# Routed attention and a gated MLP on one core: the second maxima step's mask pass beside the scores in 32-row tiles, `bounded` next to `shifted`, and the routing maxima in the score bank

## The chip, the cores and the metric

The kernel runs on one core of a Trainium2 chip. The metric is the time of one execution in device microseconds (us). A measurement of it can tell about 0.2% from no change. The engines are named as in the profile: PE (TensorE matmuls; PEld its weight loads), DVE (VectorE), ACT (ScalarE), POOL (GpSimd), SP (SyncE, which issues DMAs).

## The reference

Two blocks in a row. The first is attention with routing: queries and keys are each assigned to the nearest of 16 centroids of their head (by cosine), and a query attends only to keys of its own cluster. The second is an MLP whose hidden layer is gated by `h * erf(softplus(h))`.

```python
# q, k, v: (4, 8, 768, 64); centroids: (8, 16, 64); float32
q_assign = argmax(einsum('bhsd,hcd->bhsc', normed(q), normed(centroids)), -1)
k_assign = argmax(einsum('bhsd,hcd->bhsc', normed(k), normed(centroids)), -1)
scores = where(q_assign[..., :, None] == k_assign[..., None, :], q @ k.T / sqrt(64), -1e9)
attn = exp(scores - scores.max(-1)); attn /= attn.sum(-1) + 1e-9
x = (attn @ v) as (3072, 512)
h = x @ w_in                                  # (512, 2048)
out = (h * erf(softplus(h))) @ w_out          # (2048, 512)
```

## The kernel before

The first 420 us or so are attention, the rest is the MLP (a Strassen-like scheme of seven block products, which the diff does not touch). The weights of the MLP are loaded during attention as 64-bit words whose conversion to float is done by hand, step by step, on ACT, DVE and POOL.

**Pairs, units, periods.** Attention works on 16 pairs of heads. The two heads e = 0, 1 of a pair lie on partitions 0 to 63 and 64 to 127, so each matmul on one head uses a 64-row tile of the array and the two heads' matmuls can stand side by side. A pair has 12 units: `half` (384 of the 768 queries) times `j` (a tile of 128 keys). One call of `period(p, i)` emits two units, `u` and `u + 1`; a pair has six periods, i = 0 to 5. Instructions issued through `te`, `ve`, `ae`, `ge` stay on their engine in the order in which the program emits them; the DMAs on `nc.sync` are placed by the scheduler.

**What a period emits on PE, in order.** At i = 0 and 3 first `turn` (six small matmuls that turn the row minima). Then the first maxima step `step_ahead(u)`; `products(u)` and `products(u + 1)` (f32, `qT` by `kT`, into two banks of a tile named `sc`); the second maxima step `step_ahead(u + 1)`; `scores(u)` and `scores(u + 1)` (bf16, `qm` by `km`, added onto the products); at i = 3 the `similarities` of the pair after next; and `attend` of the two units of the period before (f32, `pr` by `v`, into a bank named `turned`). ACT's `curve` takes the exponential of an `sc` tile into `pr`. There are two `sc` tiles, used in turn.

**Masks.** For each head, `km` and `qm` (bf16, 64 rows by 768) hold, in rows 0 to 15, a penalty of -BIG for each cluster that is not the key's, and a one for the query's cluster; in row 32 (`SH`), a one for the key and the shift of the query. Their product is the mask plus the shift, so `scores` adds both at once. `pick` spreads the one-hot rows `hotT` into these places (`masks`), and `nbig` is the bias of the `km` conversion. `MASKS` says in which periods, and at which of four places in a period, a mask is made.

**Maxima.** A maxima step (12 for each pair, made half a pair ahead) gives an upper bound of the masked scores of 128 queries over 384 keys: two passes into the tile `wide` (two banks, one for each head; there is a single such tile), first `qv` by `kv` (bf16 copies of q and k), then `qm` by `km`, the mask; DVE reduces `wide` over its 768 columns into `nmx`. After six steps DVE reduces `nmx` into `lowest`, and `turn` brings the result into row 32 of `qm`. The next step can overwrite `wide` only after the reduction.

**Routing.** `choose` runs in period 3: DVE transposes the similarities into `sims`, reduces each group of 16 to its maximum `mx`, which stands in 24 spare columns (488 to 511) of `wide`'s first bank, compares (`hot`), and in period 5 transposes `hot` into `hotT`.

**Weights.** For each of 22 early weight pieces: ACT's `size_and_rest`, DVE's `bounded` (a maximum with 2.0), DVE's `shifted` (a shift by 3) with ACT's `sign`, POOL's `summed`. Two pieces are in work in each pair.

In the profile all instructions carry the line of the recording helper (L63), so groups are told apart by the names of their tiles: `wide<-kv,qv` and `wide<-km,qm` are the passes of the maxima steps, `sc<-qT,kT` (or `sc<-more_out`, every third pair, whose q and k lie in `more_out`) the products, `sc<-qm,km` the scores, `turned<-pr,in_v` the attends, `turned<-hotT,pick` a mask, `turned<-lowest,identb` the warming matmuls of the set-up.

Of the kernel before, what the change touches and what calls it, by code (L numbers as in the profile page):

```python
# [20 lines left out]
B, H, S, D = 4, 8, 768, 64  # L21
C = 16
NJ = S // P
Q = 32
# [4 lines left out]
NPAIR = B * HP  # L29
# [14 lines left out]
BIG = 2.0**60  # L44
FLOOR = 2.0**50
EPS = 2.0**-70
SH = 2 * C
NPT = NJ + 2
N_LATE = 10
LAST_X = 11  # L50
# [21 lines left out]
def kernel(  # L72
# [168 lines left out]
    def bounded(n):  # L241
        w = w_steps[n][0]
        ve.tensor_scalar(out=w, in0=w, scalar1=2.0, scalar2=None, op0=ALU.max)
# [5 lines left out]
    def shifted(n):  # L249
        w = w_steps[n][0].bitcast(U32)  # L250
        ve.tensor_scalar(out=w, in0=w, scalar1=3, scalar2=None, op0=ALU.logical_shift_left)
# [6 lines left out]

    ve.memset(nbig, 0.0)
    for e in range(2):  # L260
        ve.memset(nbig[e * D : e * D + C], -BIG)
        ve.memset(nbig[e * D + SH : e * D + SH + 1], 1.0)
    for t in maxima:
        ve.memset(t, FLOOR)
    ve.memset(pick, 0.0)
# [58 lines left out]
    def choose(p, spare=None):  # L324

        if p >= NPAIR:
            return
        st = pairs[p]
        n = HW // C
        sims = routep.tile([P, HW], F32, name="sims")  # L330
        ve.transpose(out=sims, in_=st.pop("psim"))
        yield
        sim = sims.rearrange("p (g c) -> p g c", c=C)
        mx = (wide[:, 0] if spare is None else spare)[:, 512 - n :]
        ve.reduce_max(out=mx, in_=sim, axis=AX.X)
        yield
        hot = routep.tile([P, HW], BF16, name="hot")
        ve.tensor_tensor(
            out=hot.rearrange("p (g c) -> p g c", c=C), in0=sim,
            in1=mx.unsqueeze(2).to_broadcast([P, n, C]), op=ALU.is_equal,  # L340
        )
        yield
        st["hotT"] = routep.tile([P, HW], BF16, name="hotT")
        ve.transpose(out=st["hotT"], in_=hot)
# [2 lines left out]
        if p < NPAIR:  # L347
            ae.copy(out=pairs[p][nm + "v"], in_=pairs[p][nm + "T"])

    def masks(p, nm, half, bank):  # L350

        if p >= NPAIR:
            return lambda: None
        st = pairs[p]
        cols = slice(half * HW, (half + 1) * HW)
        r = slice(0, D) if nm == "q" else slice(D, P)
        won = bank[:, 0:HW]
        te.matmul(won, lhsT=pick[r, half], rhs=st["hotT"][r], start=True, stop=True)
        if nm == "q":
            return lambda: ae.activation(out=st["qm"][:, cols], in_=won, func=ACT.Relu)  # L360
        return lambda: ae.activation(
            out=st["km"][:, cols], in_=won, func=ACT.Identity, bias=nbig, scale=BIG
        )

    turns = []

    def maxima_step(p, i, sm=wide):

        st = pairs[p]
        nmx = maxima[p % 2]  # L370
        t, half = divmod(i, 2)
        for a, b, start in (("qv", "kv", True), ("qm", "km", False)):
            for e in range(2):
                r = slice(e * D, (e + 1) * D)
                te.matmul(
                    sm[:, e, 0:HW], lhsT=st[a][r, t * P : (t + 1) * P],
                    rhs=st[b][r, half * HW : (half + 1) * HW], start=start, stop=not start,
                )
        ve.tensor_reduce(
            out=nmx[:, :, t, half], in_=sm[:, :, 0:HW], axis=AX.X, op=ALU.max, negate=True  # L380
        )
        if i in (NJ - 1, 2 * NJ - 1):
            h = i // NJ
            ve.tensor_reduce(
                out=lowest[h][:, :, SH::D].rearrange("p t e -> p e t"),
                in_=nmx[:, :, h * HJ : (h + 1) * HJ], axis=AX.X, op=ALU.min,
            )
            turns.append((p, h))

    def turn(p, h, copies=(ae.copy, ae.copy)):  # L390

        st = pairs[p]
        pn = turned[h][:, 0:HW].rearrange("p (t n) -> p t n", t=HJ)
        for t in range(HJ):
            for e in range(2):
                cols = slice(e * D, (e + 1) * D)
                te.matmul(pn[cols, t], lhsT=lowest[h][:, t, cols], rhs=identb, start=True, stop=True)
        for e, copy in zip(range(2), copies):
            r = slice(e * D + SH, e * D + SH + 1)
            copy(out=st["qm"][r, h * HW : (h + 1) * HW], in_=pn[r].rearrange("p t n -> p (t n)"))  # L400
        st["shift", h] = True

# [20 lines left out]
    def scores(u):  # L423

        p, half, j = units[u]
        st = pairs[p]
        sc = sc_of[u]
        assert ("shift", half) in st
        for e in range(2):
            r = slice(e * D, (e + 1) * D)  # L430
            te.matmul(
                sc[:, e, 0:HW], lhsT=st["km"][r, j * P : (j + 1) * P],
                rhs=st["qm"][r, half * HW : (half + 1) * HW], start=False, stop=True,
            )
# [270 lines left out]
    def run(work):  # L705
        for _ in work:
            pass

    def step_ahead(u):
        p, i = divmod(u + NJ, 2 * NJ)
        if p < NPAIR:
            maxima_step(p, i)

    forms = sum((left_forms(ve, *w_in_parts(f, 2)) for f in range(0, HF, 2)), [])
    routing = [iter(())]
# [2 lines left out]
    def period(p, i):  # L720
        u = 2 * NJ * p + 2 * i
        n1, n2 = 2 * p - 1, 2 * p
        early = lambda n: 0 <= n < N_EARLY

        def mask(place):
            which = (MASKS if p else FIRST_MASKS).get((i, place))
            if which:
                return masks(p + 1, *which, turned[0 if i in (0, 5) else 1])
            return lambda: None

        if u > 0:
            for which in turns if i in (0, 3) else ():
                turn(*which)
                turns.remove(which)
            step_ahead(u)
        mask(0)()
        next(part[0], None)
        if u == 2:
            next(routing[0])
        products(u)  # L740
        products(u + 1)
        mask(1)()
        if u > 0:
            step_ahead(u + 1)
        next(part[0], None)
        scores(u)
        scores(u + 1)
        later = mask(2)
        if i == 3:
            similarities(p + 2)  # L750
            routing[0] = choose(p + 2)
        curve(u)
        later()
        curve(u + 1)
        if u == 0:
            step_ahead(1)
            similarities(1)
            routing[0] = choose(1, turned[0])
            next(routing[0])
            next(routing[0])  # L760
            vectors(1, "q")
            vectors(1, "k")
        if i == 0 and early(n1 - 1):
            shifted(n1 - 1)
            sign(n1 - 1)
        elif i == 1 and early(n1):
            size_and_rest(n1)
        elif i == 2 and early(n1):
            bounded(n1)
        elif i == 3 and early(n1):  # L770
            shifted(n1)
            sign(n1)
        elif i == 4 and early(n2):
            size_and_rest(n2)
        elif i == 5 and early(n2):
            bounded(n2)
        for work in forms[: FORMS.get(p, {}).get(i, 0)]:
            work()
            forms.remove(work)
        if i == 3:  # L780
            for _ in range(3):
                next(routing[0], None)
        if i == 0:
            if p:
                transposes(p + 2, "q")
        elif i == 1:
            load(p + 1, "v", v, vp)
            if p == 0:
                run(routing[0])
                transposes(2, "q")  # L790
        elif i == 2:
            transposes(p + 2, "k")
        elif i == 4:
            vectors(p + 2, "k")
        elif i == 5:
            run(routing[0])
            vectors(p + 2, "q")
        if u > 0:
            for w in (u - 2, u - 1):
                accumulate(w)  # L800
            if i == 1 and early(n1 - 1):
                summed(n1 - 1)
            elif i == 4 and early(n1):
                summed(n1)
            for w in (u - 2, u - 1):
                attend(w)
            if i % HJ == 0:
                part[0] = divide(u - 1)
                next(part[0])
        mask(3)()  # L810
# [25 lines left out]
    for r in (0, D):  # L836
        for half in range(2):
            for e in range(2):
                c = r + half * Q + e * C
                ve.tensor_copy(  # L840
                    out=pick[r : r + D, half, e * D : e * D + C], in_=first[r : r + D, c : c + C]
                )
    also = ps_s.tile([P, 2, 512], F32, name="sc", tag="s")
    products(0)
# [11 lines left out]
    for n in range(PLACES - 1):  # L856
        fetch(n)
    for i in range(NJ):
        maxima_step(0, i, also if i % 2 else wide)
        if i == 1:  # L860
            masks(0, "q", 1, turned[1])()
        if i < NJ - 1:
            warm(2, turned[0], zeros)
# [125 lines left out]
```

## Time and profile before

| | |
|---|---|
| time, median of 3 runs | 1015.37 us (1015.36 to 1015.42) |
| the profiled execution: time, span | 1015.54 us, 1013.8 us |
| granted PE clock | 1.000 |
| busy: PE, PEld, DVE, ACT, POOL | 1006.4, 724.0, 695.5, 513.5, 346.5 us |
| `wide<-kv,qv` 64*128 64x384 bf16 | x378, 69.4 us busy |
| `wide<-km,qm` 64*128 64x384 bf16 | x378, 68.3 us busy |
| `sc<-qm,km` 64*128 64x384 bf16 | x384, 53.7 us busy |
| 46 to 342 us: busy DVE, ACT, POOL of 296 us | 228.75, 236.47, 227.76 us |

A shape such as 64*128 is the tile of the array (rows by columns), 64x384 the moving operand. Busy times count an overlap of two matmuls once. The ends of matmuls are modelled, so the distance between starts says more than a length. "Waits" are the times in which an engine stood idle before an instruction that a semaphore of another engine released last.

### The profile page before, as it was taken

The page shows a single profiled execution, that of the slowest core. Times are in us where ns is not written, and L with a number is a line of the kernel's source. Part 1 is how long each engine was busy: PE and PEld are TensorE (multiplying, and loading weights), DVE is VectorE, ACT ScalarE, POOL GpSimd, SP SyncE. Part 2 cuts the span into 40 slices and gives each one's busy share as a digit, 9 for nine tenths or more (in the row PEclk, how much of TensorE's full clock was granted, in tenths as well). Part 3 has the DMA queues.
Part 4 walks back from the last instruction along what each step waited for, and adds up shares of the span by engine and source line. Part 5 has one row for each costly group of instructions (what it writes and reads, how often), then busy time and mean ns, then how long its engine had stood idle before and what let it go on. Part 6 is the DMA issues. An engine that isn't in the chain of part 4 may idle for free.

```text
span 1013.8 us, 15440 instructions
## 1 busy us (share of the span) xinstructions
PE 1006.4 (99%) x5930; PEld 724.0 (71%) x5930; DVE 695.5 (69%) x1305; ACT 513.5 (51%) x673; POOL 346.5 (34%) x229
## 2 busy tenths in 40 slices
PE   8999999999999999999999999999999999999998
PEld 3555555555555555488888888888888888888887
DVE  8777777777777777879766564756565647565753
ACT  3788888888887666467714232222324150505050
POOL 1777777777777667844030000000000000000000
PEclk9999999999999999999999999999999999999999
DMA  9344444444344311052000100110001000000001
GB/s 218 67 103 100 99 103 104 105 105 105 83 105 104 63 32 33 16 174 68 17 1 33 51 1 1 42 42 1 18 24 42 1 22 22 1 1 21 21 1 41
DMA packets 141641, 55.55 MB, mean 55 GB/s; under 512 B 127104, under 2 KB 131456, under 8 KB 141568
## 3 DMA queue, kind: packets, MB, share of 16 engines
q1 hardware_dynamic: 139216, 54.28, 20.9%
q8 instruction: 46, 0.75, 0.3%
q10 hardware_dynamic: 2352, 0.30, 0.2%
q14 instruction: 27, 0.22, 0.1%
HBM read 41.98 MB, written 12.58 MB: 54 GB/s over the span
## 4 chain that ended last, share of the span: by engine, by line
PE 97%; DVE 1%; DMA 1%; POOL 0%; ACT 0%; SPq 0%; issue 0%; DVEq 0%; ACTq 0%; POOLq 0%
PE bank L63 43%; PE turned L63 32%; PE sc L63 15%; PE wide L63 7%; DVE nmx L63 1%; POOL more_out L63 0%; DMA in_k<-in_k_dram 0%; DMA in_q<-in_q_dram 0%; DVE kT L63 0%; SPq L63 0%; DVE sims L63 0%; ACT inv L63 0%; DVE qT L63 0%; ACT pr L63 0%; DVE den L63 0%
## 5 line engine op out<-in xcount | busy, mean ns | idle before, releaser
L63 POOL TENSOR_TENSOR more_out<-more_out,pr 128x768 f32<-128x768 f32 x128 | 224.0, 1750 | 68.0 <-ACT pr L63 62.9
L63 DVE TENSOR_REDUCE nmx<-wide 128x2 f32<-128x768 f32 x189 | 180.7, 956 | 88.6 <-PE wide L63 64.3
L63 ACT ACTIVATE pr<-sc 128x768 f32<-128x768 f32 x192 | 147.1, 810 | 78.1 <-PE sc L63 78.1
L63 PE MATMUL turned<-pr,in_v 128*64 128x386 f32 x768 | 145.4, 500 | 0.1
L63 DVE TENSOR_TENSOR g<-bank,g 128x256 f32<-128x256 f32 x222 | 89.5, 421 | 53.2 <-PE bank L63 46.7
L63 PE MATMUL bank<-x_own,w_in 128*128 128x256 f32 x424 | 104.5, 380 | 0.0
L63 PE MATMUL bank<-w_out,g 128*128 128x256 f32 x448 | 103.1, 379 | 0.0
L63 PE MATMUL sc<-qT,kT 64*128 64x384 f32 x528 | 99.7, 484 | 0.0
L63 PEld LDWEIGHTS turned<-pr,in_v 128*64 128x64 f32 x768 | 46.6, 136 | 69.8 <-issue 65.1
L63 PEld LDWEIGHTS bank<-w_out,g 128*128 128x128 f32 x448 | 85.1, 190 | 11.6
L63 PEld LDWEIGHTS bank<-x_own,w_in 128*128 128x128 f32 x424 | 80.3, 190 | 12.2 <-issue 1.2
L63 ACT COPY g<-bank 128x256 f32<-128x256 f32 x28 | 10.4, 372 | 152.2 <-PE bank L63 148.2
L63 DVE TENSOR_TENSOR osb<-bank,osb 128x256 f32<-128x256 f32 x87 | 35.4, 419 | 72.8 <-ACT osb L63 25.4
L63 ACT ACT_TABLE_LOAD x48 | 61.6, 1283 | 45.9 <-DVE g L63 40.9
L63 POOL TENSOR_TENSOR more_out<-pr,pr 128x768 f32<-128x768 f32 x32 | 59.1, 1847 | 50.0 <-ACT pr L63 38.5
L63 PE MATMUL bank<-x_more,more_in 128*128 128x256 f32 x296 | 76.0, 379 | 0.0
L63 PEld LDWEIGHTS <-qv 64*128 64x128 bf16 x384 | 25.6, 93 | 65.2 <-issue 51.0
L63 PE MATMUL wide<-kv,qv 64*128 64x384 bf16 x378 | 69.4, 328 | 1.1 <-ACT km L63 0.6
L63 PE MATMUL wide<-km,qm 64*128 64x384 bf16 x378 | 68.3, 322 | 0.0
L63 PEld LDWEIGHTS sc<-qT,kT 64*128 64x128 f32 x528 | 56.2, 187 | 16.6 <-issue 1.2
L63 PE MATMUL bank<-more_out,g_more 128*128 128x256 f32 x272 | 64.3, 379 | 0.0
L63 DVE TENSOR_TENSOR g<-a_s,g 128x512 f32<-128x512 f32 x96 | 62.4, 687 | 1.4 <-ACT a_s L63 1.4
(162 smaller groups left out, 1704.8 us busy)
## 6 DMA issues: line engine op xcount, KB each, us to landing
x_own<-in_moe_w_in_dram SPq DMA_DIRECT2D x13, 512.0 KB, 4.0
in_v<-in_v_dram SPq DMA_DIRECT2D x32, 192.0 KB, 2.9
x_dram<-more_out SPq DMA_DIRECT2D x32, 192.0 KB, 2.2
x_own<-x_dram SPq DMA_DIRECT2D x6, 1024.0 KB, 5.1
out_dram<-osb SPq DMA_DIRECT2D x23, 256.0 KB, 2.0
in_k<-in_k_dram SPq DMA_DIRECT2D x59, 96.0 KB, 2.6
in_q<-in_q_dram SPq DMA_DIRECT2D x58, 96.0 KB, 3.1
g_more<-in_moe_w_out_dram SPq DMA_DIRECT2D x6, 512.0 KB, 3.4
```

The costliest lines, as they stand in the source:

```text
L63: ins = getattr(self.engine, name)(*args, **kw)
```

## The change

Three things.

1. Each head's 64 mask rows become two copies of a 32-row block: row 0 the shift (first copy) or nothing, rows 1 to 16 the clusters, row 32 nothing, rows 33 to 48 the clusters again. `scores` uses rows 0 to 31 of each head, a 32-row tile. The second maxima step of a period (`behind`) uses rows 32 to 63 for its mask pass, also a 32-row tile, and that pass is emitted after `scores(u)` instead of before it. First maxima steps still use all 64 rows (the penalty then counts twice). Masks made at a place after the scores use 32 rows of `hotT`.
2. `bounded` of a weight piece moves from period 2 to period 3, or from period 5 to period 0 of the next pair, directly ahead of `shifted`.
3. `choose` puts `mx` into the spare columns of the tile of `sc` that `scores(u + 1)` has just filled, in place of `wide`'s. The reduction that writes it then waits for ACT's exponential of that tile, and the next products into that tile wait for `hot`.

In the built program PE has the same instructions in another order; DVE has four more memsets of `nbig` (eight small ones after the first) and its eight copies into `pick` are twice as long.

```diff
-SH = 2 * C
...
     for e in range(2):
-        ve.memset(nbig[e * D : e * D + C], -BIG)
-        ve.memset(nbig[e * D + SH : e * D + SH + 1], 1.0)
+        for n in range(2):
+            r = e * D + n * Q
+            ve.memset(nbig[r : r + C + 1], -BIG)
+            ve.memset(nbig[r : r + 1], 1.0 - n)
...
-    def masks(p, nm, half, bank):
+    def masks(p, nm, half, bank, narrow=False):
...
         r = slice(0, D) if nm == "q" else slice(D, P)
+        if narrow:
+            r = slice(r.start + half * Q, r.start + (half + 1) * Q)
...
-    def maxima_step(p, i, sm=wide):
+    def maxima_step(p, i, sm=wide, behind=False):
...
-        for a, b, start in (("qv", "kv", True), ("qm", "km", False)):
+
+        def passes(a, b, start, rows):
             for e in range(2):
-                r = slice(e * D, (e + 1) * D)
+                r = slice(e * D + rows.start, e * D + rows.stop)
                 te.matmul(
                     sm[:, e, 0:HW], lhsT=st[a][r, t * P : (t + 1) * P],
                     rhs=st[b][r, half * HW : (half + 1) * HW], start=start, stop=not start,
                 )
+
+        passes("qv", "kv", True, slice(0, D))
+        if behind:
+            yield
+        passes("qm", "km", False, slice(Q, D) if behind else slice(0, D))
...
-                out=lowest[h][:, :, SH::D].rearrange("p t e -> p e t"),
+                out=lowest[h][:, :, ::D].rearrange("p t e -> p e t"),
...
-            r = slice(e * D + SH, e * D + SH + 1)
+            r = slice(e * D, e * D + 1)
             copy(out=st["qm"][r, h * HW : (h + 1) * HW], in_=pn[r].rearrange("p t n -> p (t n)"))
...
             r = slice(e * D, (e + 1) * D)
+            r = slice(r.start, r.start + Q)
             te.matmul(
                 sc[:, e, 0:HW], lhsT=st["km"][r, j * P : (j + 1) * P],
...
-    def step_ahead(u):
+    def step_ahead(u, behind=False):
         p, i = divmod(u + NJ, 2 * NJ)
-        if p < NPAIR:
-            maxima_step(p, i)
+        steps = maxima_step(p, i, behind=behind) if p < NPAIR else iter(())
+        if not behind:
+            run(steps)
+        return steps
...
-                return masks(p + 1, *which, turned[0 if i in (0, 5) else 1])
+                return masks(p + 1, *which, turned[0 if i in (0, 5) else 1], place > 1)
...
         mask(1)()
-        if u > 0:
-            step_ahead(u + 1)
+        second = step_ahead(u + 1, True) if u > 0 else iter(())
+        next(second, None)
+        scores(u)
+        next(second, None)
         next(part[0], None)
-        scores(u)
         scores(u + 1)
         later = mask(2)
         if i == 3:
             similarities(p + 2)
-            routing[0] = choose(p + 2)
+            routing[0] = choose(p + 2, sc_of[u + 1][:, 0])
...
         if i == 0 and early(n1 - 1):
+            bounded(n1 - 1)
             shifted(n1 - 1)
             sign(n1 - 1)
         elif i == 1 and early(n1):
             size_and_rest(n1)
-        elif i == 2 and early(n1):
+        elif i == 3 and early(n1):
             bounded(n1)
-        elif i == 3 and early(n1):
             shifted(n1)
             sign(n1)
         elif i == 4 and early(n2):
             size_and_rest(n2)
-        elif i == 5 and early(n2):
-            bounded(n2)
...
                 ve.tensor_copy(
-                    out=pick[r : r + D, half, e * D : e * D + C], in_=first[r : r + D, c : c + C]
+                    out=pick[r : r + D, half, e * D : (e + 1) * D].rearrange("p (n c) -> p n c", n=2)[:, :, 1 : C + 1],
+                    in_=first[r : r + D, c : c + C].unsqueeze(1).to_broadcast([D, 2, C]),
                 )
...
-        maxima_step(0, i, also if i % 2 else wide)
+        run(maxima_step(0, i, also if i % 2 else wide))
```

## The prediction

> **What bounds the kernel now.** I read the page first: busy shares, the forty slices, the chain that ended last.
>
> ```profile
> PE 1006.4 (99%) x5930; PEld 724.0 (71%) x5930; DVE 695.5 (69%) x1305; ACT 513.5 (51%) x673; POOL 346.5 (34%) x229
> PE   8999999999999999999999999999999999999998
> PEclk9999999999999999999999999999999999999999
> PE 97%; DVE 1%; DMA 1%; POOL 0%; ACT 0%; SPq 0%; issue 0%; DVEq 0%; ACTq 0%; POOLq 0%
> ```
>
> TensorE is busy in every slice at the full granted clock and carries 97% of the chain. The other engines matter only where a semaphore of theirs holds TensorE. So I read the waits of PE; the row on the maxima is
>
> ```profile
> PE wide L63 <- DVE nmx L63: 0.4, 2, 0.2
> ```
>
> PE waits in total for 4.1 us, nearly all in the set-up. The attention stage (to about 420 us) is a packed sequence of matmuls, and an edit there is worth what it does to the spacing of their starts. Next, then, the timeline of PE over one period (start, length of the merged group):
>
> ```profile
> 306.61 0.34 PE L63 MATMUL wide<-kv,qv 64*128 64x384 bf16 x2
> 306.78 0.33 PE L63 MATMUL wide<-km,qm 64*128 64x384 bf16 x2
> 306.94 1.45 PE L63 MATMUL sc<-more_out 64*128 64x384 f32 x8
> 308.23 0.33 PE L63 MATMUL wide<-kv,qv 64*128 64x384 bf16 x2
> 308.40 0.33 PE L63 MATMUL wide<-km,qm 64*128 64x384 bf16 x2
> 308.56 0.49 PE L63 MATMUL sc<-qm,km 64*128 64x384 bf16 x4
> 308.98 1.52 PE L63 MATMUL turned<-pr,in_v 128*64 128x386 f32 x8
> 310.43 0.34 PE L63 MATMUL wide<-kv,qv 64*128 64x384 bf16 x2
> ```
>
> The two heads' 64-row matmuls run side by side: x2 takes 0.33, one matmul's length. I call such a side-by-side group a pass. Eight f32 matmuls, four passes, take 308.23 − 306.94 = 1.29; bf16 passes follow each other at half of an f32 pass, 0.162 us. From the first scores to the attends is 0.42, not 2 × 0.162 = 0.32: where the tile shape goes from 64*128 to 128*64, 0.10 is lost, and again on the way back. Every change of shape in the trace has this gap; nearest to a change in the number of rows alone, between bf16 matmuls, is the set-up, where warming matmuls of 128*128 alternate with maxima steps:
>
> ```profile
> 13.86 0.34 PE L63 MATMUL wide<-kv,qv 64*128 64x384 bf16 x2
> 14.03 0.33 PE L63 MATMUL wide<-km,qm 64*128 64x384 bf16 x2
> 14.29 0.50 PE L63 MATMUL turned<-lowest,identb 128*128 128x384 bf16 x2
> 14.72 0.34 PE L63 MATMUL sc<-kv,qv 64*128 64x384 bf16 x2
> ```
>
> One cycle of four passes takes 14.72 − 13.86 = 0.86, of which the passes are 4 × 0.162 = 0.65: two changes of shape cost 0.21, one 0.107.
>
> **Part 1, the mask pass beside the scores.** Removed from the path: one bf16 pass, 0.162, where the second maxima step's mask pass (rows 32 to 63 of each head) starts with `scores(u)` (rows 0 to 31): four matmuls into four banks (`wide`'s two, `sc`'s two). Added: a change from 64-row to 32-row tiles, between the `kv,qv` pass and the scores, that was not there. The change to the attends existed before. The `k` mask of place 2 is narrowed too and stays in the 32-row stretch, so no change back is added. Cost of the new change: bounds are 0 (32-row tiles inside the same columns count as no change of shape) and 0.14 (64*128 to 128*64, where the first attend pass, at 0.375 against 0.325, adds 0.05 to its 0.09 gap). I take 0.107, from the nearest row. Saved per period: 0.162 − 0.107 = 0.055.
>
> Do four row tiles run at full rate? No row shows four. Bounds: the pass stays 0.162, or the two pairs run one after the other, 0.324. Four tiles side by side exist by columns: the similarities,
>
> ```profile
> 291.13 0.52 PE L63 MATMUL turned<-qT,ccT 128*32 128x384 f32 x2
> 291.14 0.52 PE L63 MATMUL turned<-kT,ccT 128*32 128x384 f32 x2
> 291.48 0.49 PE L63 MATMUL turned<-qT,ccT 128*32 128x384 f32 x2
> ```
>
> where four start within 0.02 and the next four come 0.35 later, against 0.32 for two. I take full rate.
> The Trainium skill speaks against it: "TensorE: Matmul & The Clock Gate", section "Measured speedup vs the span model", gives 3.07 times for four row tiles of K=32, not 4. By that figure a pass of four would take an estimated 0.21, and the sum would end at about no change; the same section's span model, some 4 ns for each further tile, would leave the sum as it is.
>
> How many: second steps exist for u = 2 to 184, 92 periods. The one at u = 2 waits for DVE in the set-up's tail and gains nothing. In pairs 12 and 13 (the two waits above, at 342.13 and 368.05) a weight form and the 0.97 transposition stand before the next reduction; there the reduction starts later by the new change and PE arrives sooner, so DVE's chain sets the time: +0.1 each. The rest: 89 × 0.055 = −4.9. The periods without a second step (u = 0, and 186 to 190) pay the change alone: 4 × 0.107 = +0.4.
>
> **Part 2, `bounded` beside the shift.** It costs nothing on PE and moves 0.33 of DVE (0.42 long, starts overlapping) to where there is room. Why it is needed shows at period 2:
>
> ```profile
> 287.99 0.42 DVE L63 TENSOR_SCALAR w_out<-w_out 128x512 f32<-128x512 f32 x1
> 288.32 0.97 DVE L63 STREAM_TRANSPOSE kT<-in_k 128x768 f32<-128x768 f32 x1
> 289.30 0.96 DVE L63 TENSOR_REDUCE nmx<-wide 128x2 f32<-128x768 f32 x1
> 293.33 0.55 DVE L63 TENSOR_TENSOR hot<-sims,wide 128x384 bf16<-128x384 f32 x1
> ```
>
> The reduction ends at 290.26 and PE's second step, which overwrites `wide`, starts at 290.39: 0.13 of slack. After the change the previous reduction starts 0.10 later and PE comes 0.055 earlier, which eats 0.16. With `bounded` gone 0.33 comes back. Where it goes: in period 3, hot ends at 293.88 + 0.33 + 0.10 = 294.31, and DVE is wanted next at 294.55 − 0.06 = 294.49; slack 0.18. In period 0 the transposition of q starts at 305.50 and ends 306.47; + 0.43 is 306.90 against the reduction due at 307.15 − 0.06: slack 0.19. Without that cover, one overrun of 0.1 in each of 12 pairs is 1.2 us. What waits on the moved operations: the sign bits' sum on GpSimd, one period later, after two additions of 1.7; no cost.
>
> **Part 3, the maxima in the score bank.** Before, PE's first step of period 4 (294.01) waits for hot (293.88); with + 0.43 it would stall 0.3 in each pair. In the score bank the wait moves to `products(u + 1)` of period 4, at 294.99 − 0.06, against hot at 294.31: 0.6 of slack. New: the reduction into that bank waits for ScalarE's second exponential, which ends at 292.67 (291.16 + 1.51); the reduction comes at 292.74 + 0.43. Queued behind it on DVE are hot and the next maxima; nobody waits. Cost 0.
>
> **Part 4, set-up.** Four more tiny memsets ahead of `identb` on DVE: five take 0.46, so + 0.4 there; PE's warming starts that much later, and the transposed centroids come late for a DVE that is busy with q until 6.19: + 0.1 to + 0.4. Eight copies into `pick` are twice as long in elements (0.75 for eight): + 0.1. Together 0 to 0.6; I take 0.3.
>
> **Sum.** −4.9 + 0.4 + 0.2 + 0.3 = −4.0. The profiled execution took 1015.54 us (span 1013.8), 0.17 above the median of 1015.37; so 1015.37 − 4.0 = 1011.4. What a measurement of this kernel can tell from no change is about 0.2%, 2.0 us.
>
> **Rivals.** *The change of rows is free.* Then 89 × 0.162 − 0.5 = 13.9 saved: 1001.5. For it: the columns stay. Against: every change of shape in the trace costs 0.09 or more. Chance 0.10, with the cases between it and the forecast.
> *Four tiles run at less than full rate, or DVE eats the gain* (the slacks of 0.18 are a few hundredths wrong and three periods of a pair lose their 0.055, 2 us): 1013.4 to 1017.4. Chance 0.13.
> *Slower: the two pairs do not overlap at all.* Place: behind the `kv,qv` pass of each period. The mask pass then takes its 0.162 as before, and 96 changes of shape are added: 96 × 0.107 + 0.5 = +10.8, 1026.2. It decides from a pass of four longer than 0.162 + 0.055 − 0.9/89 = 0.207: above that the kernel loses. A new change of shape of 0.17 does the same (96 × 0.17 − 92 × 0.162 + 0.5 = +1.9). For it: no row with four row tiles or a 32-row tile. Against: two row tiles and four column tiles both run at the rate of one. Chance 0.17.
>
> **How the numbers follow.** The forecast, 1008 to 1013.4, has 0.60. Range: 1003.5 to 1017.5; left out are the free change's end (some 0.07) and the slower case beyond it (0.12). Faster 0.60 + 0.10 = 0.70, same 0.13, slower 0.17.
>
> **What would show it.** In a period like that at 306.61: from the second `kv,qv` pass to the scores 0.26 to 0.27 where 0.33 was, with `km,qm` starting within 0.02 of the first two scores; then 0.17 to the second scores, 0.25 to the attends; 3.82 becomes 3.76. The waits of PE should name `nmx` no more than two or three times. Scores 0.16 behind `kv,qv` would mean a free change; second scores 0.3 behind the first would mean tiles in turn; a row of waits on DVE of some 40 entries would mean that the cover is gone. A time under 1006 or over 1015 proves the 0.107 or the full rate wrong.

## The result, and the profile after

The changed kernel takes 1023.02 us (six runs, 1022.54 to 1024.84) against 1015.40 (1015.36 to 1015.47): ratio 1.0077, 95% interval 1.0064 to 1.009. It is 7.6 us slower where 4.0 faster was forecast. The profiled execution took 1022.54 us, with a span of 1020.8 against 1013.8. Its page:

```profile
PE 1005.0 (98%) x5930; PEld 705.8 (69%) x5930; DVE 709.7 (70%) x1309; ACT 508.6 (50%) x673; POOL 340.9 (33%) x229
PE 93%; DVE 5%; issue 1%; DMA 0%; SPq 0%; ACT 0%; DVEq 0%
```

PE is busy for less time than before (1005.0, from 1006.4), and DVE has come into the chain that ended last: 5% where it had 1%. The mechanism on PE is what the prediction said. The timeline of PE over the period that answers to the one shown of before:

```profile
305.93 0.34 PE L62 MATMUL wide<-kv,qv 64*128 64x384 bf16 x2
...
307.55 0.33 PE L62 MATMUL wide<-kv,qv 64*128 64x384 bf16 x2
307.81 0.34 PE L62 MATMUL sc<-qm,km 32*128 32x384 bf16 x2
307.82 0.34 PE L62 MATMUL wide<-km,qm 32*128 32x384 bf16 x2
307.98 0.32 PE L62 MATMUL sc<-qm,km 32*128 32x384 bf16 x2
308.24 1.52 PE L62 MATMUL turned<-pr,in_v 128*64 128x386 f32 x8
309.69 0.34 PE L62 MATMUL wide<-kv,qv 64*128 64x384 bf16 x2
```

The scores start 0.26 behind `kv,qv`, the mask pass within 0.01 of them, the second scores 0.17 later, the attends 0.26 after that. The period takes 309.69 − 305.93 = 3.76, as forecast, where it took 3.82. But two kinds of waits eat this and more. The first kind is in the waits of PE:

```profile
PE wide L62 <- DVE nmx L62: 6.4, 9, 1.6
PE turned L62 <- DVE hotT L62: 1.0, 3, 0.3
```

From the first attends of a pair to those of the next, the trace has 25.80 us for pairs 1 to 10 (25.83 before), but 26.99, 28.39, 28.38 and 26.28 for pairs 11 to 14, where before had 25.83, 25.92, 25.92 and 24.88. Together these four lose 7.5 us; the rest of the run is 0.5 shorter, and the two profiled spans differ by 7.0. Pairs 11 to 14 are those whose periods 2 and 5 hold a weight form, a DVE addition of two SBUF operands (a form adds or subtracts blocks of weights, or later of x, for the MLP). There are seven such forms: before, they take 0.68 each; after, all seven take 2.12. In period 5 the transposition into `hotT` stands behind the form, hence the second row of waits. DVE in period 2 of pair 12, after:

```profile
339.14 0.96 DVE L62 TENSOR_REDUCE nmx<-wide 128x2 f32<-128x768 f32 x1 [0.96 <-PE wide L62]
340.22 2.12 DVE L62 TENSOR_TENSOR w_in<-w_in 128x512 f32<-128x512 f32 x1
342.26 0.96 DVE L62 STREAM_TRANSPOSE more_out<-in_k 128x768 f32<-128x768 f32 x1
343.16 0.92 DVE L62 TENSOR_REDUCE nmx<-wide 128x2 f32<-128x768 f32 x1
```

and ACT, POOL (x2 merges two additions) and PE at the same time:

```profile
339.15 0.81 ACT L62 ACTIVATE pr<-sc 128x768 f32<-128x768 f32 x1 [1.29 <-PE wide L62]
340.11 3.77 POOL L62 TENSOR_TENSOR more_out<-more_out,pr 128x768 f32<-128x768 f32 x2 [0.49 <-ACT pr L62]
344.13 0.34 PE L62 MATMUL wide<-kv,qv 64*128 64x384 bf16 x2 [1.56 <-DVE nmx L62]
```

The same place before, DVE and then ACT and POOL:

```profile
338.58 0.96 DVE L63 TENSOR_REDUCE nmx<-wide 128x2 f32<-128x768 f32 x1 [0.82 <-PE sc L63]
...
339.66 0.68 DVE L63 TENSOR_TENSOR w_in<-w_in 128x512 f32<-128x512 f32 x1
```

```profile
338.80 0.81 ACT L63 ACTIVATE pr<-sc 128x768 f32<-128x768 f32 x1 [1.35 <-PE sc L63]
339.75 3.88 POOL L63 TENSOR_TENSOR more_out<-more_out,pr 128x768 f32<-128x768 f32 x2 [0.55 <-ACT pr L63]
```

Before, the form started 0.09 ahead of POOL's addition and took 0.68; the addition took 2.13 of the 3.88. After, the form starts 0.11 behind the addition, which takes 1.68, and ends 0.55 after it has ended: 2.12. The maxima reductions and the 768-column transpositions beside the same additions keep their 0.92 to 0.97. POOL begins 0.14 after ACT's exponential of the period's first unit, in both kernels. DVE begins after its maxima reduction. Before, the mask pass ran a pass ahead of the scores, and the reduction ended 0.07 before that exponential; now both matmul passes run side by side, and it ends 0.13 after. A shift of 0.2 us on an engine with idle time lost a race, and the next reduction, and PE's second step behind it, came 1.6 us late (343.16 + 0.92, PE at 344.13).

The second kind does not stand in the waits by its name, only in PE's timeline: `minus` begins 0.60 behind the last attend pass in period 3 of pairs 1 to 11, where 0.32 is a pass and what it was before. DVE there:

```profile
316.12 0.96 DVE L62 TENSOR_REDUCE nmx<-wide 128x2 f32<-128x768 f32 x1 [0.83 <-PE wide L62]
316.99 0.88 DVE L62 TENSOR_SCALAR w_out<-w_out 128x512 f32<-128x512 f32 x2
317.79 0.57 DVE L62 STREAM_TRANSPOSE sims<-turned 128x384 f32<-128x384 f32 x1
```

and PE:

```profile
316.88 1.52 PE L62 MATMUL turned<-pr,in_v 128*64 128x386 f32 x8
318.51 0.87 PE L62 MATMUL turned<-more_out,minus 128*64 128x384 f32 x4
```

`sims` reads the similarities from the bank `turned[1]`, and `minus` writes its sums into that bank. With `bounded` and `shifted` (0.88) ahead of it, `sims` ends at 318.36, and PE, due at 318.23, starts 0.15 after that. This costs 0.28 in each of 11 pairs, and the four `minus` matmuls behind the late start take 0.80 up to the next `kv,qv` in place of 0.75. Together that is 0.33 a pair, 3.6 us (pair 11 is in the 7.5 too), and leaves 0.03 of the 0.35 that a pair saves.

### The profile page after: what moved, and what is told of

It reads as the page before. It is cut to its first block, busy times and chain, and to the rows that moved or that the text cites. A ratio compares the mean times of both kernels' runs of the same rounds, so it can differ in the third digit from the quotient of the medians.

```text
span 1020.8 us, 15472 instructions
## 1 busy us (share of the span) xinstructions
PE 1005.0 (98%) x5930; PEld 705.8 (69%) x5930; DVE 709.7 (70%) x1309; ACT 508.6 (50%) x673; POOL 340.9 (33%) x229
## 4 chain that ended last, share of the span: by engine, by line
PE 93%; DVE 5%; issue 1%; DMA 0%; SPq 0%; ACT 0%; DVEq 0%
PE bank L62 43%; PE turned L62 31%; PE sc L62 15%; PE wide L62 5%; DVE nmx L62 2%; DVE more_in L62 1%; DVE w_in L62 1%; DMA in_k<-in_k_dram 0%; DVE kT L62 0%; SPq L62 0%; DVE hotT L62 0%; DVE lowest L62 0%; DVE sims L62 0%; DVE qT L62 0%; DVE more_out L62 0%
## 5 line engine op out<-in xcount | busy, mean ns | idle before, releaser
L62 POOL TENSOR_TENSOR more_out<-more_out,pr 128x768 f32<-128x768 f32 x128 | 218.5, 1707 | 68.0 <-ACT pr L62 62.8
L62 PE MATMUL wide<-km,qm 64*128 64x384 bf16 (+1 forms) x378 | 62.5, 327 | 0.0
```

What stands on the lines that cost most here:

```text
L62: ins = getattr(self.engine, name)(*args, **kw)
```

## The experiments

Theories: **A**, a DVE operation with two SBUF inputs, or a `tensor_scalar`, that starts after a POOL addition is held until that addition ends. **M**, `bounded` ahead of `sims` delays the bank that `minus` overwrites. Rivals are named in the expectations. The ratio and its 95% interval are against the kernel before on the same chip, which took 1015.5 to 1015.8.

**Forms moved** (changed kernel, table of forms alone).

```diff
-    11: {5: 1}, 12: {0: 1, 2: 1, 5: 1}, 13: {0: 1, 2: 1, 5: 1}, 14: {0: 2, 2: 1, 3: 1, 5: 1},
-    15: {0: 1, 2: 1, 3: 2, 4: 2, 5: 2},
+    12: {0: 2, 3: 1}, 13: {0: 2, 3: 1}, 14: {0: 2, 3: 2},
+    15: {0: 2, 3: 3, 4: 2, 5: 3},
```

> The changed kernel with the weight forms (two-input additions on DVE) of pairs 11 to 14 taken out of periods 2 and 5 and put into periods 0 and 3 and into pair 15; all else as in the changed kernel. Theory A (a form that starts after GpSimd has begun its addition is held until that addition ends: 2.12 us in place of 0.68, and the next maxima reduction and PE's second step behind it): no form in pairs 12 to 14 takes over 1 us, pairs 12 and 13 fall from 28.4 to about 26 us, and the time from 1023.0 to about 1016 (up to 1018 if the forms pushed into pair 15 delay the end of attention). Rival B (the forms are slow because DVE has too much work, wherever they stand): the time stays at 1022 to 1024.

Measured: 1015.33 us (ratio 0.9998, 0.9988 to 1.0007). The twelve forms up to the middle of pair 15 take 0.68 or 0.69 each; pairs 12 and 13 take 25.83 and 25.61. DVE has the same 1309 instructions as in the changed kernel, so B falls.

**Form first** (changed kernel; in periods 2 and 5 of all pairs but the last, the forms stand ahead of the reduction into `lowest`).

```diff
-    def maxima_step(p, i, sm=wide, behind=False):
+    def maxima_step(p, i, sm=wide, behind=False, between=lambda: None):
...
+        between()
         if i in (NJ - 1, 2 * NJ - 1):
             h = i // NJ
...
+        early_forms = i in (2, 5) and p < NPAIR - 1
+        second = step_ahead(u + 1, True, between=some_forms if early_forms else lambda: None) if u > 0 else iter(())
```

> The changed kernel with one thing moved: in periods 2 and 5 the form stands directly behind the maxima reduction, ahead of the small reduction into lowest, in place of behind it. It then starts some 0.2 us earlier, at about 0.09 before the reduction's end, and GpSimd's addition starts at about the reduction's end. Theory A (who starts first holds the other up): the forms take 0.68 again, GpSimd's addition beside them gets 0.4 to 0.6 longer, the stalls of 2.0 and of 0.8 + 0.8 us in pairs 12 and 13 go, a new wait of PE's turn for lowest of up to 0.35 each comes, and the time is 1016 to 1018. Rival B (too much work on DVE): nothing was taken from DVE, so 1022.5 to 1023.5.

Measured: 1016.79 us (1.0013, 1.0003 to 1.0022). In the same period 2 of pair 12, DVE and then POOL:

```profile
339.86 0.68 DVE L62 TENSOR_TENSOR w_in<-w_in 128x512 f32<-128x512 f32 x1
```

```profile
339.96 3.88 POOL L62 TENSOR_TENSOR more_out<-more_out,pr 128x768 f32<-128x768 f32 x2 [0.48 <-ACT pr L62]
```

The form starts 0.10 ahead, takes 0.68, and POOL is the longer one again. No work was removed and none changed engine; what changed is who came first. The price is the predicted wait for `lowest`: 1.5 us in 8 places, of which one of 0.2 stood in the changed kernel already.

**Bounded back** (changed kernel, part 2 undone).

```diff
         if i == 0 and early(n1 - 1):
-            bounded(n1 - 1)
             shifted(n1 - 1)
...
+        elif i == 2 and early(n1):
+            bounded(n1)
         elif i == 3 and early(n1):
-            bounded(n1)
...
+        elif i == 5 and early(n2):
+            bounded(n2)
```

> The changed kernel with bounded back at periods 2 and 5 (part 2 undone), parts 1 and 3 kept. Theory A: bounded, a one-input operation of 0.42, now also starts after GpSimd's addition; if it is held up as the forms are, it ends 1.2 us later in 22 places and PE stalls about 1.1 to 1.3 in each: some 24 us more, less 3.1 for the stall of minus that goes, so about 1044. Rival C (only operations with two inputs in SBUF are held up, and part 2 merely relieves DVE's queue): the stall of 0.28 at minus goes from 11 pairs, and period 2 stalls by a few hundredths: 1020 to 1021.

Measured: 1045.54 us (1.0296, 1.0281 to 1.0311), 1.5 over A's figure. A row of its DVE in period 5, one of POOL, and its wait on the maxima:

```profile
293.84 1.87 DVE L62 TENSOR_SCALAR w_out<-w_out 128x512 f32<-128x512 f32 x1
```

```profile
293.73 3.52 POOL L62 TENSOR_TENSOR more_out<-more_out,pr 128x768 f32<-128x768 f32 x2 [0.47 <-ACT pr L62]
```

```profile
PE wide L62 <- DVE nmx L62: 26.2, 31, 1.6
```

A `tensor_scalar` with one input is held too (1.87 in place of 0.42), so C falls. With part 1 in place, part 2 is worth 22 us; not for DVE's room, as the prediction had it, but because in periods 3 and 0 POOL is idle when `bounded` starts (its next addition comes 0.7 later).

**Parts 2 and 3 alone** (kernel before, with `bounded` in periods 3 and 0 and the routing maxima in the score bank).

> The kernel before with parts 2 and 3 alone (bounded beside shifted, maxima of the routing in the score bank); masks in 64-row tiles, maxima steps as before. Theory A: the reduction still ends before GpSimd begins, so no form takes over 1 us in pairs 12 and 13. Theory M (bounded ahead of sims on DVE delays the reading of the similarities' bank, which PE's minus matmul then overwrites): sims ends 0.45 later than before, against a slack of 0.41, so a stall of some 0.04 in 11 pairs. Together 1015.4 to 1016.2. Rival D (part 2 costs its 0.28 per pair whatever the order of PE): 1018.5. Rival E (the forms are slow because of parts 2 or 3): over 1020.

Measured: 1016.58 us (1.001, 1.0001 to 1.002). This is 0.4 above the expected range. The gap at `minus` is 0.365, a stall of 0.05, as M has it; forms take 0.68 to 0.74 before pair 15. A pair takes 25.93, 0.10 more than before: the stall is one half, and the four `minus` matmuls behind it, again 0.80 in place of 0.75, are the other. D and E fall.

**Bounded on GpSimd** (changed kernel).

```diff
+    def bounded_aside(n):
+        w = w_steps[n][0]
+        ge.tensor_scalar(out=w, in0=w, scalar1=2.0, scalar2=None, op0=ALU.max)
...
         if i == 0 and early(n1 - 1):
-            bounded(n1 - 1)
             shifted(n1 - 1)
...
         elif i == 3 and early(n1):
-            bounded(n1)
             shifted(n1)
...
                 accumulate(w)
+            if i in (2, 5) and early(n1 if i == 2 else n2):
+                bounded_aside(n1 if i == 2 else n2)
```

> The changed kernel with bounded done by GpSimd, behind its two additions of periods 2 and 5, in place of by DVE beside the shift. DVE has 0.42 less ahead of sims in period 3. Theory M (DVE's bounded ahead of sims delays the bank that minus overwrites): the gap of 0.60 between attends and minus falls to 0.32 in pairs 1 to 11, a pair takes 25.5 in place of 25.8, and the time falls by 3 us to about 1020, the stalls in pairs 11 to 14 being left. Rival F (minus waits for something else than the reading of the similarities): the gap of 0.60 stays, 1023.

Measured: 1021.87 us (1.0062, 1.0047 to 1.0077), where about 1020 was expected. The gap falls from 0.60 to 0.50, not to 0.32. GpSimd needs 1.48 for its `bounded`, which pushes its additions into period 3, and now `shifted` is held there (0.79 in place of 0.42). So F falls, and about a third of the stall is gone.

**Both**, the two before together.

> The changed kernel with bounded done by GpSimd (as in the run before) and the forms out of periods 2 and 5 of pairs 11 to 14. If theories A and M are the whole loss, what is left is the saving of part 1, 0.05 for each of 92 periods: 1015.4 - 4.6 = about 1011 (1010 to 1013, by what the forms pushed into pair 15 cost there). If something else of the change costs time too, it stays above 1014.

Measured: 1014.19 us (0.9985, 0.9975 to 0.9995). This lies above the expected 1010 to 1013. A pair takes 25.71, where the shift-later run below reaches 25.47: what is left of M, 0.24 in 11 pairs, is 2.6 of the 3.2 us that are missing.

**Control: the forms moved in the kernel before** (the table of "Forms moved" alone).

> The kernel before with the forms alone moved out of periods 2 and 5 (the same table as in the runs with moved forms), nothing else changed: the control for those runs. Theory A: in the old order the forms are not held up, so moving them gains only the two waits of 0.075 us on the maxima and costs or gains some tenths at the end of attention: 1014.8 to 1015.8. If the forms' place is worth over 1 us in the old order too, what the runs with moved forms gained is not owed to the changed order of PE.

Measured: 1016.59 us (1.0011, 1.0002 to 1.0019), outside the expectation: in the old order that table costs 1.1 us, 0.3 in attention and 0.7 in the MLP, where PE waits 0.5 for x's forms. So by itself the table gains nothing; what it gains in the changed kernel hangs on the changed order.

**Shift later** (both of the above, but the first piece's `bounded` on DVE in period 3, its shift in the next pair's period 0, both sums in period 1; `bounded` of the second piece stays on GpSimd).

```diff
         if i == 0 and early(n1 - 1):
-            bounded(n1 - 1)
+            if early(n1 - 2):
+                shifted(n1 - 2)
             shifted(n1 - 1)
...
         elif i == 3 and early(n1):
             bounded(n1)
-            shifted(n1)
```

> The changed kernel with the forms out of periods 2 and 5 of pairs 11 to 14, bounded of the first piece of a pair on DVE in period 3 without its shift, that shift in period 0 of the next pair (beside the second piece's shift), both pieces' sums in period 1, and bounded of the second piece on GpSimd in period 5. In period 3 DVE then has one 0.42 operation ahead of sims, as in the kernel before, and it starts while GpSimd is free or late. Theory M: the gap between attends and minus is 0.32 in all pairs, a pair takes 25.5 us, and the time is 1012 (1011.5 to 1013), 0.3% under the kernel before. If GpSimd's two sums in period 1 push its additions onto DVE's operations, a pair takes 25.7 or more and the time stays at 1014 or above.

Measured: 1013.65 us (0.9987, 0.9978 to 0.9995), above the expected 1011.5 to 1013. In this run and the next the last early piece's sum was made after x had been loaded into its buffer, so that piece's weights are not the reference's. M holds in full: the gap is 0.32, a pair takes 25.47. But pairs 11 and 12 take 27.7 and 27.5. In pair 11 it is shift and two forms in one period 0: the second form is held for 2.19, and PE stands for 2.01 us. In pair 12 no form is held (0.68 or 0.69 each): from 333.6 to 337.0 us, beginning 1.4 after that stand ended, the granted clock is 0.50, and eight attend matmuls take 2.17 in place of 1.52. The executions of this kernel lie at 1013.4 to 1013.7 or at 1014.7 to 1015.2, and the kept trace is of the second kind.

**Set-up** (the same, `nbig`'s memsets behind the copy into `identb`).

> The shift-later kernel with one more edit: the memsets of nbig stand behind the copy into identb on DVE in the set-up, not ahead of it. The nine memsets hold up identb by about 0.8 us, so PE's warming begins 0.8 us earlier. If the set-up's length hangs on it, the first attends start at 24.4 or earlier and the time falls by 0.3 to 0.6; if it hangs on the loads and DVE's own chain, nothing changes (within 0.2).

Measured: 1013.23 us (0.9983, 0.9974 to 0.9992). The copy into `identb` starts 0.8 us earlier, but the first warming matmuls only 0.5 (1.89, from 2.38); the first attends start at 24.43 (24.71 in the run before). That is no proof: the changed kernel itself, without this edit, has 24.45, and the forms-moved run with the changed kernel's set-up 25.08. Here too the executions lie at two places, 1013.0 to 1013.2 and 1014.6 to 1014.7, the lower one 0.4 under that of the run before. The kept trace is of the first kind: it has the same stand of 2.01 us, no fall of the clock, and pair 12 at 25.84. So in 10 of the 22 executions of these two kernels the stand seems to have cost a second time, 1.3 to 1.8 us; that it caused the fall of the clock is not shown, but the two kernels below, which have no such stand in attention, show no such executions among 13.

**Last piece** (the same, but piece 21 shifted in period 3 and summed in period 4 of pair 11).

> The set-up kernel (run before) with the last early weight piece as in the changed kernel: bounded and shifted in period 3 of pair 11, its sum in period 4 (in the two runs before, that piece's sum was made after x had been loaded into its buffer, so that the piece's weights were not the reference's). The shift in period 0 of pair 12, ahead of two forms, goes; there a form was held up and PE stood 2.0 us for the maxima. Theory A: that wait goes, pair 11 to 12 falls from 27.7 to about 26.1 us, and the time from 1013.2 to 1011.4 (1011 to 1012), 0.4% under the kernel before. Rival: the 2.0 us come from the two forms themselves; then nothing changes.

Measured: 1011.75 us (0.9961, 0.9948 to 0.9973), the best of all: 4.0 us under the kernel before on the same chip (1015.76). That this is the forecast's 4.0 is in part chance, since the table of forms, the place of `bounded` and the set-up differ from the changed kernel's. The page's first row and the waits that are left on the maxima:

```profile
PE 1002.0 (99%) x5930; PEld 704.6 (70%) x5930; DVE 697.1 (69%) x1298; ACT 508.9 (50%) x673; POOL 357.2 (35%) x240
```

```profile
PE wide L62 <- DVE nmx L62: 0.6, 3, 0.2
```

Pairs 1 to 10 take 25.48 (25.83 before): 0.35 in six periods, 0.058 each. Pair 11 falls to 26.15, as theory A has it, so the rival falls.

**Fewer forms in period 0** (the same, one form less there in pairs 12 and 13, two more in pair 15).

> The last-piece kernel with one form less in period 0 of pairs 12 and 13 (two more in pair 15, periods 4 and 5). If DVE's queue in period 0 (two forms ahead of the transposition of q) is what makes pair 11 to 12 longer than 25.5, some 0.3 us each go: 1010.8 to 1011.2. If pair 15 pays for the two forms more, with x's forms late for the MLP's first products, the time is 1011.5 to 1012.5.

Measured: 1012.92 us (0.9971, 0.9961 to 0.9982). Pairs 11 and 12 gain 0.35 and 0.23, as expected, but in the kept trace (of the longest execution, 1013.35) the MLP takes 1.6 longer, where PE stands 1.6 for a form of x (`x_more`): pair 15 pays, as the second expectation says. The first attends also start 0.67 later there (25.23), which this edit does not touch; that would account for the time being above even 1012.5.

## Why the prediction was wrong, point by point

- *Part 1 on PE*: right. A change from 64 to 32 rows costs 0.093 in start distance (0.255 against 0.162; forecast 0.107 with what follows it), four row tiles run at the rate of two (they start within 0.01, and the next pass comes 0.17 after the first of them, as it does after two at a change of shape), and a period saves 0.058 (0.055). The Trainium skill's factor of 3.07 for four row tiles ("TensorE: Matmul & The Clock Gate", "Measured speedup vs the span model") does not show in these passes of 384 columns; the same section's span model fits them. The skill also says that changing the tiling mode drains the array ("TensorEngine Tiling (Array Packing)", "Key Properties"). The 0.093 fits that, for a change of rows alone; the drain itself does not stand in a trace.
- *The step that failed*: pairs 12 and 13, "+ 0.1 each", and pairs 11 and 14, nothing. That term took a form's 0.68 as fixed and moved only the starts. The forms measured 2.12, and the four pairs lost 7.5 us where the sum had them gain 1.0. I priced the mask pass's place by PE and by DVE's queue, and never asked what else starts when the first scores are done: ACT's exponential, and 0.14 after it POOL. The trace of before showed both sides: POOL's additions at 2.13 beside a form and 1.68 elsewhere, forms of 2.17 in pair 15. The Trainium skill says it in "SBUF — State Buffer", "Who interferes with whom": DVE and GpSimd share a pair of ports, a DVE operation with two SBUF inputs or a `tensor_scalar` in a two-port mode contends for it, whoever issues first holds it for the whole instruction, and a `tensor_reduce` never contends. The prediction did not draw on it. The runs agree in which operations are held and that the order decides (0.68 to 2.12, 0.42 to 1.87, reductions at 0.92 to 0.96); that a port is what they share, no trace shows.
- *Part 2, "It costs nothing on PE"*: the second step that failed, by 3.6 us. I followed `hot` and the next reduction, but not who waits for the bank that `sims` reads. The 0.33 was also too small: beside each other, `bounded` and `shifted`, which reads its result, take 0.88, 0.46 more than `shifted` alone. In the old order the slack of 0.41 covers all but 0.05 of it.
- *Part 3*: right; no products waited for `hot`.
- *Set-up, + 0.3*: the first attends of the changed kernel start 0.11 earlier than before, not later. Kernels with the same set-up edits lie between 24.45 and 25.1; why is open.
- *The rivals*: "DVE eats the gain" named the right engine, but its price (2 us) came from slacks of hundredths in a queue and not from a neighbour on GpSimd. The slower rival was the wrong mechanism, and its 1026 only happens to lie near 1023.
- *What would show it*: the forecast of PE's distances, 3.76 a period, came true, while PE waited nine times on the maxima in place of two or three. A time over 1015 was to prove the 0.107 or the full rate wrong; both held, and that sign was itself wrong.

## What to carry to other kernels

When an edit moves a pass on the bounding engine by 0.2 us, list everything that its end releases on every engine, and ask of each two operations that start within some tenths of each other whether they share something; whether a cover holds is then a matter of order, not of idle time. A duration from the trace holds for the neighbours it had there: look at an instruction's spread, and at which of its neighbours the long ones had. Before putting work ahead of an operation on a queue with room, find who overwrites what that operation reads.

## What the runs showed of the hardware

A 0.68 us DVE addition becomes 2.12 if a 1.68 us GpSimd addition began 0.11 us before it, and stays 0.68 if it begins 0.09 us ahead of it, at GpSimd's expense (2.13). A one-input `tensor_scalar` of 0.42 is held the same way (1.87). GpSimd's own `tensor_scalar` on 128x512 f32 took 1.48 us, DVE's 0.42. In one trace the granted clock of PE was 0.50 for 3.4 us, beginning 1.4 us after PE had stood idle for 2.01; in another the same stand was followed by no fall.
